# Attention in front of two expert layers: last rows, last key chunk and softmax factors as 128x128 tiles, and a scheduler that counts changes of TensorE's tiling

## The chip, the cores and the metric

One Trainium2 chip, one core, one launch. The metric is the device time in microseconds of one execution of the whole program. Four engines compute: TensorE (PE), VectorE (DVE), ScalarE (ACT) and GpSimd (POOL); SyncE (SP) issues most of the transfers. Each engine takes its own instructions in program order and waits on semaphores for the others.

## The reference

Three layers in a row, all float32. The attention is local softmax attention mixed with a memory read; its output is the input of a mixture of experts, whose output goes through a gated layer.

```python
B, H, S, D = 4, 8, 576, 64
scores = where(causal, -1e9, q @ k.T / sqrt(D));  scores -= scores.max(-1)
a = exp(scores);  a /= a.sum(-1) + 1e-9
local = a @ v
q_p = phi(q)                                  # phi(x) = where(x > 0, x, exp(x) - 1) + 1
mem = (q_p @ M_prev) / (q_p . z_prev + 1e-6)
out = g * mem + (1 - g) * local               # g = sigmoid(beta), one per head
x = moe(out as 2304 rows of 512)              # 8 experts, one per row, width 1024
y = (sigmoid(x @ w_gate) * (x @ w_val)) @ w_out   # width 1536
```

## The kernel before, in words

**Attention** works on 16 pairs of heads (`pi` 0 to 15; two pairs make a load group `gi`). A head has 576 rows: four chunks of 128 and a last one of 64. The last 64 rows of two heads are laid on the two halves of the partitions of one 128x128 tile; the two pairs of a load group stand side by side in an array of 18 blocks of 64 columns, whose last 128 columns (`1024:1152`) hold the last rows of pair `l` in the partitions `64*l` to `64*l+63`. Per pair, the steps are:

- `turn` (L309 to L322): q, k and phi(q) are transposed on TensorE, chunks 0 to 2 as group 0, chunks 3 and 4 as group 1. Chunks of 128 rows are 128x128 transposes (L316), the last one uses 64 partitions only (L320), the half that belongs to the pair. `q_part`, `z_part`, `k_part`, `p_part` take the result out of PSUM, q and k as a high part (ACT) and a low part (DVE).
- `scores` (L368): for chunks 0 to 3 of the rows, two heads side by side, each with 64 contraction rows (L378, six matmuls); for the last rows both heads at once with 128 contraction rows (L385).
- `masked` and `exp`: DVE masks and takes the maximum out of PSUM (L407), ACT exponentiates and sums (L415).
- `turn_probs`, `keep_probs`: 128x128 transposes of the probabilities (L460), copied out of PSUM by ACT or DVE (L304, L306). The last key chunk gives 64 rows.
- `recip`, `rc_turn`, `rc_copy`, `fan`: 1/sum of each row (18 columns: nine high, nine low) is transposed (L432) into `rT` of 18 partitions and spread over the partitions by matmuls with a selecting matrix `pick` of 18 contraction rows (L444, L446).
- `out_part` (L494): probabilities times v, the two heads writing the two halves of the output partitions, 64 weight columns each; the last key chunk has 64 contraction rows. `mem_part` (L480) reads the memory. `out_scale`, `out_add` (DVE) combine.

So TensorE is used in several **tilings**: whole (128x128), two row halves (64 contraction rows: L378, L320), two column halves (64 output partitions: L494), column halves on 64 rows (L494's last chunk), 18 rows (L444, L446), and 32 columns (L833, the router's logits).

**Order.** The order of all steps, on all engines, is made by a list scheduler (`Plan`, L55). A step has a rank, a cost for each engine that may run it, needs, and buffers that it takes and uses. `order` picks again and again the ready step with the smallest key: first the earliest start in steps of 0.02 us by the planner's own clock, then the rank. Instructions are then issued in the order of those starts. Buffers set waits: two PSUM tiles for scores (`Sp`), four for all else (`T`).

**After attention** come the routing (ranks of the rows by expert, lists of row numbers), a gather of the first rows from memory, the experts' loop and the gated layer; these have orders of their own that no edit here touches. While attention runs, the first experts' weights are already loaded and split.

Of the kernel before, what the change touches and what calls it, by code (L numbers as in the profile page):

```python
# [20 lines left out]
HG = 4  # L21
# [31 lines left out]
def chunk_rows(c):  # L53
    return 128 if c < 4 else 64


class Plan:
# [8 lines left out]
    SAME = {"PE": 0.0, "DV": 0.13, "PL": 0.1, "AC": 0.06, "SP": 0.0, "Q": 0.0}  # L66

    def __init__(self, bufs, later, step):


        self.bufs, self.later, self.step, self.steps, self.users = bufs, later, step, {}, {}

    def add(self, name, rank, cost, fn, needs=(), takes=(), uses=()):

        assert name not in self.steps, name
        self.steps[name] = (rank, cost, fn, tuple(needs), tuple(takes))
        for t in (*takes, *uses):
            self.users.setdefault(t, []).append(name)

    def order(self):  # L80
# [6 lines left out]
        ready, out = [n for n, w in waits.items() if not w], []  # L87
# [10 lines left out]
        while ready:  # L98
            best = None
            for n in ready:  # L100
# [4 lines left out]
                for e, c in cost.items():  # L105
                    t = max([free.get(e, 0.0), *t0, *(end[m][0] + (self.SAME if end[m][1] == e and (e != "SP" or n[0] == "ld") else self.LAG)[end[m][1]] for m in needs)])
                    b_ = self.later.get(e, 0.0) if len(cost) > 1 else 0.0
                    key = (n != "cp", round((t + b_) / self.step), rank, t + c + b_)
# [4 lines left out]
            end[n], free[e] = (t + c, e), t + c  # L113
            for tag, key in self.steps[n][4]:
# [12 lines left out]
class Attention:  # L127
# [14 lines left out]
    def constants(self, beta):  # L142
# [4 lines left out]
        self.rb = cp.tile([P, S], F32, name="rb")  # L147
        self.qT = [cp.tile([P, 2, 512], F32R, name=f"qT{i}") for i in range(2)]
# [48 lines left out]
        self.pt = [cp.tile([P, 2, NK, S], F32, name=f"pt{i}") for i in range(2)]  # L197

    def choices(self):

        nc, cp, n = self.nc, self.cp, 2 * NQ
        f = self.pt[1].rearrange("p h k q -> p (h k q)")[0:n, 0 : 6 * P].rearrange("p (c m) -> p c m", m=P)
        nc.gpsimd.memset(f, 0.0)
# [8 lines left out]
        self.pick = cp.tile([n, 6, P], F32R, name="pick")  # L212
        nc.gpsimd.tensor_copy(self.pick, f)
# [42 lines left out]
    def load_v(self, gi):  # L256
        b, h0 = gi // 2, (gi % 2) * HG
        self.G[gi, "v"] = vn = self.ld.tile([P, NK, HG, D], F32, name="vn", tag="vn")
        for hh in range(HG):
# [4 lines left out]
            out=vn[:64, 4, :, :], in_=self.v[b, h0 : h0 + HG, 512:576, :].rearrange("h p d -> p h d")  # L264
# [43 lines left out]
    def turn(self, nm, pi, g):  # L308
# [4 lines left out]
        for c in self.GROUPS[g]:  # L313
# [4 lines left out]
            else:  # L318
                r = slice(l * 64, (l + 1) * 64)
                nc.tensor.transpose(T[:, n : n + 64], src[r, 1024:1152], self.ident[r, r])  # L320
                n += 64
        self.T[nm, pi, g] = T, self.GROUPS[g][0] * 128, n  # L322

# [10 lines left out]
    def z_part(self, pi, lo):  # L334

        z, T = self.z8[pi % 2], self.T["q", pi, 1][0]
        for j in range(2):
            r = slice(j * 64, j * 64 + 64)
            v = T[r, 128:192]
# [5 lines left out]
    def k_part(self, pi, g, lo):  # L345
# [3 lines left out]
        T, c0, n = self.T["k", pi, g]  # L349
        if lo:  # L350
            self.nc.vector.tensor_tensor(  # L351
                kz[:, 1, c0 : c0 + n], T[:, :n], kz.bitcast(F32)[:, 0, c0 : c0 + n], ALU.subtract
            )
        else:
# [1394 lines left out]
```

## Time and profile before

| what | us |
|---|---|
| three runs, median (lowest to highest) | 1106.94 (1103.66 to 1111.6) |
| the profiled execution, device time | 1110.49 |
| its span, first to last instruction | 1108.6 |
| TensorE busy in the span | 1028.2 (93%) |
| VectorE / ScalarE / GpSimd busy | 525.0 / 456.2 / 289.1 |

The rows of the profile below come from that one execution; 1.9 us of its time lie outside the span. TensorE's matmuls are pipelined, so the time of one row reaches into the next: what a group of matmuls costs is read from the start of its row to the start of the next row. An fp32 matmul can stand as two instructions, so counts in the trace can be twice those in the order.

### The profile page before, as it was taken

The page shows a single profiled execution, that of the slowest core. Times are in us where ns is not written, and L with a number is a line of the kernel's source. Part 1 is how long each engine was busy: PE and PEld are TensorE (multiplying, and loading weights), DVE is VectorE, ACT ScalarE, POOL GpSimd, SP SyncE. Part 2 cuts the span into 40 slices and gives each one's busy share as a digit, 9 for nine tenths or more (in the row PEclk, how much of TensorE's full clock was granted, in tenths as well). Part 3 has the DMA queues.
Part 4 walks back from the last instruction along what each step waited for, and adds up shares of the span by engine and source line. Part 5 has one row for each costly group of instructions (what it writes and reads, how often), then busy time and mean ns, then how long its engine had stood idle before and what let it go on. Part 6 is the DMA issues. An engine that isn't in the chain of part 4 may idle for free. (4 is left out here: it accounts for less than half of the span.)

```text
span 1108.6 us, 17069 instructions
## 1 busy us (share of the span) xinstructions
PE 1028.2 (93%) x6181; PEld 878.6 (79%) x6181; DVE 525.0 (47%) x1263; ACT 456.2 (41%) x1049; POOL 289.1 (26%) x396
## 2 busy tenths in 40 slices
PE   6899899999869699989979789999999999999997
PEld 4567566666559589968968689999899999999996
DVE  5877677676564163246216799931212122121111
ACT  5687686876444253236224455521212221221211
POOL 8677446231374152035115200000100100100101
PEclk9899999999879899999999889999999999999999
DMA  6637445321277164138225455500110100100000
GB/s 123 130 99 172 104 85 131 73 66 36 75 261 257 44 236 136 39 91 295 73 66 149 162 175 196 159 1 1 38 48 1 58 1 1 57 1 1 30 1 28
DMA packets 111899, 102.49 MB, mean 92 GB/s; under 512 B 69520, under 2 KB 86928, under 8 KB 111760
## 3 DMA queue, kind: packets, MB, share of 16 engines
q1 hardware_dynamic: 107888, 88.18, 27.7%
q0 software_dynamic: 3872, 12.62, 3.6%
q8 instruction: 68, 1.11, 0.4%
q14 instruction: 71, 0.58, 0.2%
HBM read 84.49 MB, written 16.28 MB: 91 GB/s over the span
## 5 line engine op out<-in xcount | busy, mean ns | idle before, releaser
L1546 DVE TENSOR_TENSOR G<-G,pT 128x384 f32<-128x384 f32 (+1 forms) x74 | 40.1, 542 | 249.0 <-PE pT L1532 247.5
L1578 POOL DMA_INDIRECT out_dram<-o,rows x18 | 17.5, 971 | 461.7 <-ACT o L1574 212.5
L1553 ACT ACTIVATE Gh<-G 128x384 fp32r<-128x384 f32 (+1 forms) x74 | 38.2, 516 | 162.1 <-DVE G L1546 162.0
L1542 ACT ACTIVATE G<-pH 128x384 f32<-128x384 f32 x72 | 35.4, 491 | 132.4 <-PE pH L1532 132.3
L415 ACT ACTIVATE Sm<-Sm,mx 128x512 f32<-128x512 f32 (+3 forms) x144 | 83.2, 579 | 14.1 <-DVE mx L407 13.6
L407 DVE CUSTOM_DVE_ANT_0 Sm<-Sp,mask 128x512 f32<-128x512 f32 (+3 forms) x144 | 65.2, 481 | 19.6 <-PE T L460 8.1
L1166 POOL TENSOR_TENSOR W<-raw,W 128x1024 fp32r<-128x1024 f32 (+1 forms) x25 | 56.7, 2274 | 66.8 <-ACT W L1159 66.8
L460 PE MATMUL T<-ident,Sm 128*128 128x128 f32 (+1 forms) x400 | 61.2, 287 | 8.9 <-ACT xt L304 3.2
L1563 PE MATMUL pX<-W,Gh 128*128 128x512 f32 x220 | 68.9, 394 | 0.0
L1159 ACT ACTIVATE W<-raw 128x1024 fp32r<-128x1024 f32 x60 | 61.7, 1054 | 13.8 <-DMA y_dram<-y 6.5
L460 PEld LDWEIGHTS T<-ident,Sm 128*128 128x128 f32 (+1 forms) x400 | 44.3, 142 | 21.0 <-ACT xt L304 4.0
L1166 DVE TENSOR_TENSOR W<-raw,W 128x1024 fp32r<-128x1024 f32 x38 | 56.9, 1508 | 6.8 <-ACT W L1159 6.8
L494 PE MATMUL O<-pt,vn 128*64 128x192 f32 (+4 forms) x512 | 59.7, 353 | 0.0
L304 ACT ACTIVATE pt<-T 128x512 f32<-128x512 f32 (+4 forms) x128 | 49.3, 434 | 24.5 <-PE T L460 24.0
L1551 DVE TENSOR_TENSOR Gl<-G,Gh 128x384 fp32r<-128x384 f32 (+1 forms) x74 | 40.4, 546 | 33.9 <-ACT Gh L1553 33.9
L1532 PE MATMUL pT<-xh,W 128*128 128x384 f32 x264 | 52.8, 343 | 2.0 <-DVE G L1546 2.0
L1532 PE MATMUL pT<-yh,W 128*128 128x384 f32 x264 | 51.3, 336 | 0.0
L378 PE MATMUL Sp<-kz,qT 64*128 64x512 f32 (+3 forms) x384 | 49.0, 361 | 1.9 <-DVE kz L351 0.8
L1532 PEld LDWEIGHTS pT<-xh,W 128*128 128x128 f32 x264 | 47.4, 192 | 3.0 <-DVE G L1546 2.2
L1297 PE MATMUL pH<-W,xh 128*128 128x512 f32 x80 | 26.4, 472 | 24.8 <-issue 24.3
L1532 PE MATMUL pH<-yh,W 128*128 128x384 f32 x240 | 47.0, 337 | 1.4 <-DVE xl L1521 1.4
L494 PEld LDWEIGHTS O<-pt,vn 128*64 128x64 f32 (+1 forms) x512 | 30.6, 137 | 21.6 <-issue 13.7
(336 smaller groups left out, 2457.8 us busy)
## 6 DMA issues: line engine op xcount, KB each, us to landing
raw<-in_moe_w_dram SPq DMA_DIRECT2D x60, 512.0 KB, 5.1
raw<-in_moe_w_gate_dram SPq DMA_DIRECT2D x12, 512.0 KB, 5.9
raw<-in_moe_w_val_dram SPq DMA_DIRECT2D x12, 512.0 KB, 3.7
raw<-in_moe_w_out_dram SPq DMA_DIRECT2D x12, 512.0 KB, 4.6
y_dram<-y SPq DMA_DIRECT2D x9, 513.0 KB, 3.5
qn<-in_q_dram SPq DMA_DIRECT2D x32, 128.0 KB, 2.6
kn<-in_k_dram SPq DMA_DIRECT2D x32, 128.0 KB, 2.7
zf<-in_z_prev_dram SPq DMA_DIRECT2D x32, 128.0 KB, 5.3
```

Of the source, the lines that this page charges most:

```text
L304: self.nc.scalar.activation(out, in_, AF.Copy)
L378: nc.tensor.matmul(Sp[:, j, 0:n], lhsT=q[r, a, c * 128 : (c + 1) * 128], rhs=kz[r, k, 0:n], start=(p_ == 0), stop=(p_ == 2), skip_group_ch ...
L407: self.nc.vector.tensor_tensor_reduce(out=self.Sm[pi, n][:, k0:k1], in0=self.Sp[pi, c][:, j if n < 8 else si, 0 : k1 - k0], in1=mask, scal ...
L415: self.nc.scalar.activation(self.Sm[pi, n], self.Sm[pi, n], AF.Exp, scale=-1.0, bias=self.mx[pi, n][:, si : si + 1], accum_out=self.sums[p ...
L460: nc.tensor.transpose(T[:kr, o * 128 : (o + 1) * 128], self.Sm[pi, n][:, i * 128 : i * 128 + kr], self.ident)
L494: nc.tensor.matmul(O[j * 64 : (j + 1) * 64, q0 - q0b : q1 - q0b], lhsT=self.G[gi, "v"][:kr, i, 2 * l + j, :], rhs=PT[:kr, j, i, q0:q1], st ...
L1159: self.nc.scalar.activation(hi, t, AF.Copy)
L1166: eng.tensor_tensor(lo[:, o : o + w], t[:, o : o + w], hi.bitcast(F32)[:, o : o + w], ALU.subtract)
L1532: nc.tensor.matmul(t, lhsT=w[:, k * P : (k + 1) * P], rhs=x[:, k, :], start=(m == k == 0), stop=(m == 2 and k == 3),)
L1546: nc.vector.tensor_tensor(t, t, p, ALU.mult)
L1551: nc.vector.tensor_tensor(l, t, hi.bitcast(F32), ALU.subtract)
L1563: nc.tensor.matmul(po[g][jj], lhsT=a[:, ts], rhs=w, start=(f == 0 and m == 0), stop=(f == NF - 1 and m == 2), skip_group_check=True,)
```

## The change

Three things are done together.

1. **Whole square tiles.** The transposes of the last rows take all 128 partitions, both pairs of the load group at once, and the pair's 64 columns are picked when PSUM is read (`turned`). So group 1 of a turn needs both halves of the load, and a copy of k or phi(q) of group 1 becomes two (128 columns and 64). The last key chunk becomes keys 448 to 575: `vn`'s chunk 4 holds 128 rows of v, the transposed probabilities keep rows 64 to 127, and rows 0 to 63 of that chunk are zeros, set once. The softmax factors' tile `rc` is 128x128 with zeros, `rT` has 128 partitions, `pick` 128 rows.
2. **Scheduler.** A TensorE step has a `mode` (0 whole, 1 row halves, 2 column halves, 3 logits). A step of another mode than the last one costs 0.12 us more in the planner and stands two ranks later.
3. **Needs.** The products `("o", pi, bk, 0)` now need the fan `("b", pi, bk)` of the same block; `recip` needs `pick`; group 1 of a turn needs load half 1.

```diff
@@ class Plan
+    CHANGE = 0.12
+    WORTH = 2.0
...
-                    key = (n != "cp", round((t + b_) / self.step), rank, t + c + b_)
+                    new = e == "PE" and self.modes[n] != tiling
+                    c += self.CHANGE * new
+                    key = (n != "cp", round((t + b_) / self.step), rank + self.WORTH * new, t + c + b_)
...
+            if e == "PE":
+                tiling = self.modes[n]
@@ constants, choices
+        self.rcs = [cp.tile([P, P], F32, name=f"rc{i}") for i in range(2)]
+        self.rT = cp.tile([P, P], F32R, name="rT")
...
+        for t in self.pt:
+            nc.gpsimd.memset(t[0:64, :, 4, 512:576], 0.0)
...
-        self.pick = cp.tile([n, 6, P], F32R, name="pick")
+        self.pick = cp.tile([P, 6, P], F32R, name="pick")
...
@@ load_v
-            out=vn[:64, 4, :, :], in_=self.v[b, h0 : h0 + HG, 512:576, :].rearrange("h p d -> p h d")
+            out=vn[:, 4, :, :], in_=self.v[b, h0 : h0 + HG, 448:576, :].rearrange("h p d -> p h d")
@@ turn
-                r = slice(l * 64, (l + 1) * 64)
-                nc.tensor.transpose(T[:, n : n + 64], src[r, 1024:1152], self.ident[r, r])
+                nc.tensor.transpose(T[:, n : n + 128], src[:, 1024:1152], self.ident)
...
+    def turned(self, nm, pi, g):
+        T, c0, n = self.T[nm, pi, g]
+        if g == 0:
+            return [(c0, T[:, :n])]
+        o = 128 + pi % 2 * 64
+        return [(c0, T[:, :128]), (c0 + 128, T[:, o : o + 64])]
@@ k_part (p_part alike)
-            self.nc.scalar.activation(kz[:, 0, c0 : c0 + n], T[:, :n], AF.Copy)
+        for c0, v in self.turned("k", pi, g):
+            c = slice(c0, c0 + v.shape[1])
+            if lo:
+                self.nc.vector.tensor_tensor(kz[:, 1, c], v, kz.bitcast(F32)[:, 0, c], ALU.subtract)
+            else:
+                self.nc.scalar.activation(kz[:, 0, c], v, AF.Copy)
@@ rc_turn, rc_copy
-        self.nc.tensor.transpose(T[0 : 2 * NQ, 0:P], self.rc[pi], self.ident)
+        self.nc.tensor.transpose(T[:, 0:P], self.rcs[pi % 2], self.ident)
...
-        self.copy(eng, self.rT[pi], self.TR[pi][0 : 2 * NQ, 0:P])
+        self.copy(eng, self.rT, self.TR[pi][:, 0:P])
@@ turn_probs, out_part
-            nc.tensor.transpose(T[:kr, o * 128 : (o + 1) * 128], self.Sm[pi, n][:, i * 128 : i * 128 + kr], self.ident)
+            k0 = min(i * 128, S - 128)
+            nc.tensor.transpose(T[:, o * 128 : (o + 1) * 128], self.Sm[pi, n][:, k0 : k0 + 128], self.ident)
...
-                O[j * 64 : (j + 1) * 64, q0 - q0b : q1 - q0b], lhsT=self.G[gi, "v"][:kr, i, 2 * l + j, :],
-                rhs=PT[:kr, j, i, q0:q1], start=(i == 0), stop=(i == last), skip_group_check=True,
+                O[j * 64 : (j + 1) * 64, q0 - q0b : q1 - q0b], lhsT=self.G[gi, "v"][:, i, 2 * l + j, :],
+                rhs=PT[:, j, i, q0:q1], start=(i == 0), stop=(i == last), skip_group_check=True,
@@ run
-                        needs=[("L", nm, gi, pi % 2)] + (before if nm == "q" else [("X", "k", pi, 0)] if g else []),
+                        needs=[("L", nm, gi, 1 if g else pi % 2)] + (before if nm == "q" else [("X", "k", pi, 0)] if g else []),
...
-                    needs = [("o", pi, bk, i - 1)] if i else [("L", "v", gi)]
+                    needs = [("o", pi, bk, i - 1)] if i else [("L", "v", gi), ("b", pi, bk)]
```

The costs that the planner gives to the split copies stay as they were.

The order of TensorE at the start of the program, before. `qn`, `kn` are loaded q and k, `Sp` scores, `Sm` probabilities, `T` a PSUM tile.

```order
L316 MATMUL T<-ident,qn 128x128 x4
L320 MATMUL T<-ident,qn 128x64
L316 MATMUL T<-ident,kn 128x128 x4
L320 MATMUL T<-ident,kn 128x64
L378 MATMUL Sp<-kz,qT_104 128x512 x6
L378 MATMUL Sp<-kz,qT_104 128x128 x6
L316 MATMUL T<-ident,qn 128x128 x4
L320 MATMUL T<-ident,qn 128x64
L460 MATMUL T<-ident,Sm 128x128 x4
```

The same place now:

```order
L330 MATMUL T<-ident,qn 128x128 x3
L330 MATMUL T<-ident,kn 128x128 x3
L330 MATMUL T<-ident,qn 128x128
L334 MATMUL T<-ident,qn 128x128
L330 MATMUL T<-ident,qn 128x128 x4
L334 MATMUL T<-ident,qn 128x128
L330 MATMUL T<-ident,kn 128x128
L334 MATMUL T<-ident,kn 128x128
L330 MATMUL T<-ident,kn 128x128 x4
L334 MATMUL T<-ident,kn 128x128
L399 MATMUL Sp<-kz,qT_107 128x512 x6
L399 MATMUL Sp<-kz,qT_107 128x128 x6
```

The first scores of the first pair stood behind that pair's transposes alone; now they stand behind the transposes of two pairs, the last of which read the second half of the load of k.

TensorE around the products of the second pair, before. `rT`, `pick` are the fan's tiles, `vn` is v, `pt` the transposed probabilities, `phT` and `MB` the memory read.

```order
L444 MATMUL T<-rT,pick 128x128 x4
L446 MATMUL T<-rT,pick 128x64 x2
L378 MATMUL Sp<-kz,qT_105 128x256 x6
L494 MATMUL O<-pt_147,vn 64x384 x2
L494 MATMUL O<-pt_147,vn 64x256 x2
L494 MATMUL O<-pt_147,vn 64x128 x2
L480 MATMUL O<-phT,MB 128x384
L494 MATMUL O<-pt_147,vn 64x192 x8
L494 MATMUL O<-pt_147,vn 64x64 x2
L460 MATMUL T<-ident,Sm 128x128 x10
```

And now:

```order
L464 MATMUL T<-rT,pick 128x128 x4
L466 MATMUL T<-rT,pick 128x64 x2
L330 MATMUL T<-ident,kn 128x128 x3
L330 MATMUL T<-ident,qn 128x128 x4
L334 MATMUL T<-ident,qn 128x128
L399 MATMUL Sp<-kz,qT_107 128x512 x6
L514 MATMUL O<-pt_150,vn 64x384 x2
L514 MATMUL O<-pt_150,vn 64x256 x2
L514 MATMUL O<-pt_150,vn 64x128 x2
L514 MATMUL O<-pt_150,vn 64x192 x8
L514 MATMUL O<-pt_150,vn 64x64 x2
L480 MATMUL T<-ident,Sm 128x128 x9
```

The products L494 of a pair, split by the memory read and with a last part on 64 rows, are now one run (L514) behind the pair's fan, and the fan stands among whole-tile steps.

## Rows read from the trace of the kernel before

**Rows 1.** The page's busy time, share of the span and instructions by engine.

```profile
PE 1028.2 (93%) x6181; PEld 878.6 (79%) x6181; DVE 525.0 (47%) x1263; ACT 456.2 (41%) x1049; POOL 289.1 (26%) x396
```

**Rows 2.** Busy time by stretch: PE, PEld, DVE, ACT, POOL, granted clock, DMA.

```profile
24.00:40.00 16.00, 13.14 (x97) 9.13 (x94) 15.29 (x53) 14.48 (x46) 7.44 (x11) 1.00 0.70 120
160.00:180.00 20.00, 19.91 (x164) 14.20 (x163) 15.98 (x59) 15.32 (x48) 8.02 (x11) 1.00 0.55 119
24.00:295.00 271.00, 255.14 (x1945) 177.25 (x1942) 196.55 (x673) 188.72 (x578) 128.07 (x173) 0.98 0.42 96
```

**Rows 3.** TensorE's timeline in mid-attention: start, us, line, output and inputs, weights, shape.

```profile
101.56 1.31 PE L460 MATMUL T<-ident,Sm 128*128 128x128 f32 x10
102.80 0.55 PE L378 MATMUL Sp<-kz,qT 64*128 64x128 f32 x6
...
103.71 0.27 PE L316 MATMUL T<-ident,qn 128*128 128x128 f32 x1
103.92 0.27 PE L320 MATMUL T<-ident,qn 64*128 64x64 f32 x1
104.12 0.33 PE L316 MATMUL T<-ident,kn 128*128 128x128 f32 x1
104.38 0.27 PE L320 MATMUL T<-ident,kn 64*128 64x64 f32 x1
104.58 0.55 PE L316 MATMUL T<-ident,ph 128*128 128x128 f32 x3
```

**Rows 4.** TensorE's timeline, three runs of scores and the rows behind them.

```profile
28.00 1.15 PE L378 MATMUL Sp<-kz,qT 64*128 64x384 f32 x12
29.08 0.55 PE L316 MATMUL T<-ident,kn 128*128 128x128 f32 x3
...
105.52 0.79 PE L378 MATMUL Sp<-kz,qT 64*128 64x384 f32 x6
106.25 0.33 PE L316 MATMUL T<-ident,ph 128*128 128x128 f32 x1
...
110.65 0.62 PE L378 MATMUL Sp<-kz,qT 64*128 64x256 f32 x6
111.20 0.55 PE L460 MATMUL T<-ident,Sm 128*128 128x128 f32 x3
```

**Rows 5.** TensorE's timeline where lines alternate and the tiling stays whole.

```profile
108.81 0.49 PE L460 MATMUL T<-ident,Sm 128*128 128x128 f32 x3
109.13 0.60 PE L930 MATMUL T<-ident,xT 128*128 128x128 f32 x4
109.57 0.49 PE L460 MATMUL T<-ident,Sm 128*128 128x128 f32 x3
```

**Rows 6.** Timeline at the start of the program, TensorE and SP's transfers.

```profile
8.22 0.79 PE L378 MATMUL Sp<-kz,qT 64*128 64x512 f32 x2 [0.42 <-ACT kz L355]
9.80 1.76 PE L378 MATMUL Sp<-kz,qT 64*128 64x512 f32 x10 [0.78 <-DVE kz L351]
...
16.08 0.61 SPq L227 DMA_DIRECT2D kn<-in_k_dram  x1
...
18.08 1.97 PE L378 MATMUL Sp<-kz,qT 64*128 64x384 f32 x12
19.98 1.12 PE L316 MATMUL T<-ident,kn 128*128 128x128 f32 x4
```

**Rows 7.** ScalarE's groups by shape, 24 to 295 us: busy, mean ns of one.

```profile
L304 ACT ACTIVATE pt<-T 128x128 f32<-128x128 f32 x24 | 5.5, 280 | 0.3 <-PE T L460 0.2
L343 ACT ACTIVATE z<-T 64x64 fp32r<-64x64 f32 x28 | 6.0, 213 | 0.2
L355 ACT ACTIVATE kz<-T 128x192 fp32r<-128x192 f32 x14 | 4.6, 328 | 0.4 <-PE T L320 0.4
```

**Rows 8.** Timeline, TensorE: the fan that waited longest.

```profile
118.72 0.52 PE L444 MATMUL T<-rT,pick 18*128 18x128 f32 x3 [1.24 <-DVE xt L306]
```

**Rows 9.** Timeline, TensorE: the first rows of the first expert.

```profile
308.76 1.09 PE L1270 MATMUL pX<-ident,xn 128*128 128x128 f32 x4 [3.25 <-DMA xn<-x_dram,kept]
```

## The prediction before the run

> **What bounds the kernel now.** I read the page first: TensorE is busy 93% of the span, no other engine half of it [rows 1]. Then the stretches. In attention, from 24 to 295 us, TensorE is busy 255.1 of 271 us, at a granted clock of 0.98, VectorE 196.6 and ScalarE 188.7, GpSimd 128.1; in a full stretch such as 160 to 180 TensorE stands at 19.91 of 20 [rows 2]. So attention is TensorE's, with one exception: from 24 to 40 us VectorE is busy 15.29 of 16 and TensorE only 13.14 [rows 2]. Behind attention comes a chain that waits for the last row of x: the first expert's transposes wait 3.25 us for the gathered rows [rows 9]. Nothing in the change touches that chain or what follows, so a microsecond won before 295 us should arrive at the end, and one lost too. The work is therefore to price attention on TensorE, then ask what the other engines give back.
>
> **What a change of tiling costs.** A group's cost is read from its start to the next row's start. Where lines alternate but the tiling stays whole, three transposes take 109.13 − 108.81 = 0.32 us and four 0.44, that is 0.107 to 0.11 each, so a new line or tile costs nothing [rows 5]. Ten transposes between two groups of scores take 102.80 − 101.56 = 1.24 us against 10 x 0.107 = 1.07: 0.17 for going in and out [rows 3]. The scores' side pays as well: widths 384 and 256 in one run take 29.08 − 28.00 = 1.08 us, apart 0.73 + 0.55 = 1.28, so 0.20 for the second out and in [rows 4]. A run of scores merged with another and the transposes between merged too saves both, 0.37 for two changes. The worst place is group 1 of the turns: whole, half, whole, half, each one transpose, from 103.71 to 104.58, 0.87 us [rows 3]. Two whole ones are 0.21; for a half one no row shows its time without the changes. It lies between 0 and 0.107, the time of a whole one; I take half, 0.053. That leaves 0.87 − 0.32 = 0.55 for four changes, 0.14 each. So the price lies between 0.085 (only the 0.17, for two) and 0.185 (0.37 for two); I take 0.14, which is also the place that the edit removes most often.
>
> **What the change removes.** Counted along TensorE's order from the first instruction to the first expert, changes between whole, row halves, column halves, 18 rows and 32 columns fall from 328 to 146. In the order of before alone, whole squares would take away 92 (the transposes of last rows 71, the fans 7, the last key chunk 14); the rest, 90, is the scheduler's: products in one run, scores behind scores. 182 x 0.14 = 25.5 us (15.5 to 33.7). The transposes of last rows get wider, 48 x 0.053 = 2.6 us back (0 to 5.1 by the bound above). Transposing `rc` whole and giving the fan and the last keys 128 contraction rows leaves the count of moving columns as it was: 0 for these, as far as the changes they caused are counted above. TensorE: −22.9 us.
>
> **What it adds.** First, the start. Scores of the first pair now need k of group 1, which needs the second half of the load. SP issues the last piece of that load at 16.08 us and the transposes that read it start at 19.98 [rows 6], against scores at 8.22 now. What TensorE did of scores before that moment, 0.79 + 1.76 + 1.97 = 4.5 us [rows 6], comes later. It costs no less than the same runs at mid-attention's speed (about half: four transposes take 1.12 us in rows 6, 0.60 in rows 5), 2.3 us, and no more than the whole shift, 19.98 − 8.22 = 11.8. VectorE, the engine that is full from 24 to 40 us, starts its masks late as well, so nothing catches up soon, but the present start also loses time waiting for the same load. I take 4.5.
>
> Second, the split copies: k high on ScalarE, k low on VectorE, phi(q) on either, one more for each of 16 pairs, 48 in all. On ScalarE 192 columns take 328 ns; 128 columns take 280 and a 64x64 piece 213 [rows 7]: 165 ns more, 48 x 0.165 = 7.9 us over two engines. They have room on average (196.6 and 188.7 of 271), but k's copies stand between its transposes and the scores. Between 0 and 7.9; half, 3.9.
>
> Third, a wait. The first product of a block now stands behind its fan, and the fan behind all nine exponentials, the reciprocal, a transpose and a copy. Queued behind it are the transposes of the next probabilities, and the copies that they feed. The longest such wait shown is 1.24 us [rows 8]. If all 16 pairs had it, 19.8 us; if the scheduler finds other whole-tile work each time, 0. I take two of that length, 2.4.
>
> More zeros to set on GpSimd and 64 more rows of v in a load of 128 KB are hidden: GpSimd is busy 128.1 of 271 us [rows 2] and v is loaded ahead of its use.
>
> **Sum.** −22.9 + 4.5 + 3.9 + 2.4 = −12.1 us. Against the profiled execution, 1110.49 (span 1108.6 and 1.9 outside), that is 1098.4. That execution lies 3.55 us above the median of 1106.94, so against the median I say **1094.8 us**, 1.1% faster.
>
> **Rivals.** *The copies become the bound.* VectorE and ScalarE together do 196.6 + 188.7 + 7.9 = 393.2 us in attention, 1.42 us per us now. Their fullest stretch under a saturated TensorE reaches 15.98 + 15.32 of 20, 1.565 [rows 2]. If no more than 1.5 can be held, attention takes 262 us instead of 271: 9 saved, less 4.5 at the start, so 4.4 and 1102.5 us. For it: from 24 to 40 us TensorE already waits for a full VectorE. Against it: on average each has over a quarter of its time free. The Trainium skill has this as a rule (TensorEngine Tiling (Array Packing), Performance Considerations, PSUM Bottleneck): what speeds TensorE up doesn't speed up emptying PSUM, which may become the bottleneck. Rows 2 bear it out for 24 to 40 us and not for 160 to 180.
>
> *The full price.* If a change costs 0.185 as two merged runs suggest, TensorE saves 31.1, and with the same 10.8 given back the gain is 20.3: 1086.6 us. For it: the second instruction behind a change is late too, which the single transposes can't show.
>
> *Slower: products wait for the fan.* Place: the first product of each pair. Price: 1.24 us in each of 16 pairs, 19.8, with the 8.4 of start and copies 28.2 against 22.9: 5.3 slower, 1112.2 us. It decides from (22.9 − 8.4) / 16 = 0.9 us per pair on. For it: the chain from the last exponential to the fan crosses three engines. Against it: one wait of 1.24 is the longest shown, and the new order puts the transposes of k, q or further scores between fan and products.
>
> *The edit doesn't do what it says*, if the time belonged to something else than the tiling, such as weights of a new tile: then fewer changes buy nothing, and only the 10.8 remain. Rows 5 speak against it, where the tile and line change four times without a price; I leave it inside the slower case.
>
> **How the numbers follow.** Forecast 0.50 (by itself 1088 to 1101), copies 0.20, full price 0.22, slower 0.08. The time is the forecast's. The range takes in the full price and the copies: **1084 to 1107**. About 1% is what a measurement of this kernel can tell from no change: below 1095.9 is faster, above 1118.0 slower. Faster is the full price and a little over half of the forecast, 0.22 + 0.28 = 0.50; slower by over 1% needs the fan's wait and the dearest start together, some part of the 0.08 and of the unknown, 0.07; the rest, 0.43, is no change that can be told.
>
> **What would show it.** Right: single transposes of last rows 0.107 us apart with no jump; products in runs; attention's last transposes some 12 us earlier; the first scores at 20 to 21 us. Wrong: a TensorE row of waits for VectorE or ScalarE well above the present 16 us idle between 24 and 295 (the copies or the fan), waits in front of the first product of a pair, or a jump at line changes in whole tiling. If the stretch behind attention changed by itself, the step that carries the gain to the end would be wrong.

## The result and the profile after

The changed kernel takes **1090.11 us**, median of 6 runs (1087.83 to 1094.44), beside 1107.15 (1103.66 to 1111.6) for the kernel before: ratio 0.9863 [0.9833, 0.9892], 17.0 us less by the medians. The forecast was 1094.8, 12.1 less. All ratios here leave out one slower run, 1113.38 us, of the kernel `order_k_first` below. The profiled execution of the new kernel took 1087.83 us, its span is 1085.8.

The page of the changed kernel, busy time by engine, against [rows 1]:

```profile
PE 1000.4 (92%) x6181; PEld 874.5 (81%) x6181; DVE 518.0 (48%) x1275; ACT 458.4 (42%) x1079; POOL 296.9 (27%) x410
```

TensorE has as many instructions as before and 27.8 us less of busy time. Where that lies is read from one landmark: the router's `T<-O,tri`, the first step that needs all of attention. It starts at 294.29 us before:

```profile
294.29 0.45 PE L951 MATMUL T<-O,tri 128*128 128x144 f32 x2
```

TensorE's timeline of the changed kernel, the places that answer to [rows 3], [rows 6], [rows 8] and [rows 9]:

```profile
15.39 0.45 PE L334 MATMUL T<-ident,qn 128*128 128x128 f32 x1 [8.15 <-DMA qn<-in_q_dram]
...
18.50 0.47 PE L334 MATMUL T<-ident,kn 128*128 128x128 f32 x1 [1.39 <-DMA kn<-in_k_dram]
...
19.98 2.18 PE L399 MATMUL Sp<-kz,qT 64*128 64x512 f32 x12
...
24.41 2.39 PE L480 MATMUL T<-ident,Sm 128*128 128x128 f32 x10
26.73 0.62 PE L399 MATMUL Sp<-kz,qT 64*128 64x256 f32 x6
...
28.18 0.49 PE L330 MATMUL T<-ident,qn 128*128 128x128 f32 x3
28.50 0.49 PE L330 MATMUL T<-ident,kn 128*128 128x128 f32 x3
...
41.42 0.27 PE L334 MATMUL T<-ident,qn 128*128 128x128 f32 x1
41.53 0.27 PE L330 MATMUL T<-ident,kn 128*128 128x128 f32 x1
41.64 0.27 PE L334 MATMUL T<-ident,kn 128*128 128x128 f32 x1
41.84 1.13 PE L399 MATMUL Sp<-kz,qT 64*128 64x128 f32 x12
...
251.79 0.66 PE L464 MATMUL T<-rT,pick 128*128 128x128 f32 x4
252.29 0.36 PE L466 MATMUL T<-rT,pick 128*128 128x64 f32 x2
252.58 2.93 PE L514 MATMUL O<-pt,vn 128*64 128x384 f32 x32
255.44 1.20 PE L480 MATMUL T<-ident,Sm 128*128 128x128 f32 x9
...
277.42 0.45 PE L971 MATMUL T<-O,tri 128*128 128x144 f32 x2
...
291.73 1.09 PE L1290 MATMUL pX<-ident,xn 128*128 128x128 f32 x4 [3.09 <-DMA xn<-x_dram,kept]
```

The transposes of last rows (L334) start 0.11 us apart, where the half ones stood 0.2 to 0.26 apart in [rows 3]. The products are one run behind the fan, and the fan waits for nothing there. The first scores come at 19.98 us; the long wait in front of them, 8.15 us, is for the second half of q, the one for k is 1.39. Attention ends at 277.42, 16.87 us earlier, and the first expert follows 17.03 earlier than in [rows 9], with nearly the same wait for its rows (3.09 us, 3.25 before).

Windows of the kernel before, up to its end of attention, and two stretches in which its granted clock fell (columns as in [rows 2]):

```profile
0.00:24.00 24.00, 13.59 (x62) 10.31 (x63) 12.25 (x54) 10.77 (x30) 20.06 (x64) 1.00 0.66 125
24.00:294.30 270.30, 254.71 (x1944) 176.96 (x1941) 196.00 (x672) 188.12 (x576) 127.45 (x172) 0.98 0.42 96
...
36.00:50.00 14.00, 12.09 (x68) 8.60 (x67) 10.58 (x39) 10.86 (x34) 11.67 (x15) 0.76 0.74 118
248.00:260.00 12.00, 9.50 (x66) 6.41 (x63) 7.95 (x33) 6.06 (x19) 5.22 (x10) 0.86 0.39 94
```

The changed kernel, its own end of attention and the stretches of [rows 2], and two that an experiment below is set against:

```profile
24.00:40.00 16.00, 14.21 (x104) 11.07 (x102) 13.58 (x54) 14.43 (x48) 8.97 (x14) 1.00 0.80 129
160.00:180.00 20.00, 19.04 (x158) 14.61 (x157) 14.31 (x55) 16.23 (x50) 9.74 (x16) 1.00 0.65 163
0.00:24.00 24.00, 8.19 (x38) 6.23 (x38) 10.66 (x45) 7.91 (x22) 21.23 (x69) 1.00 0.68 129
24.00:277.40 253.40, 236.42 (x1968) 180.66 (x1964) 191.66 (x692) 193.02 (x614) 129.67 (x182) 1.00 0.44 104
60.00:100.00 40.00, 37.20 (x312) 28.63 (x312) 33.09 (x113) 31.21 (x104) 29.21 (x39) 1.00 0.65 155
...
24.00:60.00 36.00, 31.43 (x242) 23.47 (x238) 29.43 (x109) 30.90 (x100) 26.72 (x36) 1.00 0.71 131
```

From these rows attention's end can be split into three: idle time of TensorE (length less busy), what the lower clock costs, and the rest, the work. Before, TensorE is busy 13.59 + 254.71 = 268.3 us to the end and idle 10.4 before 24 us and 15.6 after. A granted clock of 0.76 is a mean of the two levels, 2.4 and 1.2 GHz, so twice the missing share stands at 1.2: 14 x 0.24 x 2 + 12 x 0.14 x 2 = 10.1 us of attention. Half of that, 5.1, is charged to the clock, so the work is 263.2. Now TensorE is busy 244.6 us, idle 15.8 before and 17.0 after, and by the clock's column never at the low level. In [rows 2]'s stretches VectorE is no longer full from 24 to 40 us (13.58 of 16, TensorE 14.21), and from 160 to 180 TensorE has lost some of its cover (19.04 for 19.91).

So −16.9 is made of **work −18.6, start +5.4, later idle +1.4, clock −5.1**.

The column misses the start. It says 1.00 there, but in the changed kernel ten transposes from 24.41 us on take 0.23 us each and those from 28.18 on 0.107; before, four take 1.12 us in [rows 6] and 0.60 in [rows 5]. TensorE's first stretch runs at half pace in all kernels here, before up to about 23 us, now up to about 27. TensorE is busy some 13 and 11 us of it. If that pace is the low level's, about 1 us of the gain belongs to the clock and not to the work: −17.4 and −6.2. In the table below the same reading moves work by −0.4 to +1.4 us, and by 3 to 4 for half_first, k_first_warm and order_k_first.

TensorE's waits in attention, after: what it waited for, total us, times, longest. Others are left out, among them those at the start and smaller ones.

```profile
PE T L334 <- DMA qn<-in_q_dram: 8.1, 1, 8.1
...
PE T L480 <- DVE xT L524: 3.2, 4, 1.6
PE T L330 <- DVE xT L530: 2.7, 2, 2.2
PE Sp L406 <- DVE mx L428: 2.6, 3, 1.0
...
PE T L480 <- DVE kz L374: 0.9, 2, 0.6
```

No wait stands in front of a pair's first product (L514), and those for the copies of k (`kz`) are below 1 us each. ScalarE's groups by shape, 24 to 277.4 us, against [rows 7]:

```profile
L376 ACT ACTIVATE kz<-T 128x128 fp32r<-128x128 f32 x14 | 3.9, 277 | 3.0 <-PE T L334 2.9
...
L376 ACT ACTIVATE kz<-T 128x64 fp32r<-128x64 f32 x14 | 3.2, 228 | 0.0
```

A split copy of k takes 277 + 228 − 328 = 177 ns more than the whole one. Whether TensorE pays for it, even_copies below asks.

### The profile page after: what moved, and what is told of

Same layout as the page of the kernel before. It is cut to its first block, busy times and chain, and to the rows that moved or that the text cites. A ratio compares the mean times of both kernels' runs of the same rounds, so it can differ in the third digit from the quotient of the medians.

```text
span 1085.8 us, 17186 instructions
## 1 busy us (share of the span) xinstructions
PE 1000.4 (92%) x6181; PEld 874.5 (81%) x6181; DVE 518.0 (48%) x1275; ACT 458.4 (42%) x1079; POOL 296.9 (27%) x410
## 5 line engine op out<-in xcount | busy, mean ns | idle before, releaser
L1186 POOL TENSOR_TENSOR W<-raw,W 128x1024 fp32r<-128x1024 f32 (+1 forms) x25 | 59.9, 2400 | 58.5 <-ACT W L1179 58.4
L428 DVE CUSTOM_DVE_ANT_0 Sm<-Sp,mask 128x512 f32<-128x512 f32 (+3 forms) x144 | 64.5, 482 | 15.6 <-PE T L480 6.8
L480 PE MATMUL T<-ident,Sm 128*128 128x128 f32 x400 | 62.7, 285 | 7.8 <-DVE xT L524 3.2
L318 ACT ACTIVATE pt<-T 128x512 f32<-128x512 f32 (+4 forms) x138 | 55.9, 447 | 32.0 <-PE T L480 30.8
L1179 ACT ACTIVATE W<-raw 128x1024 fp32r<-128x1024 f32 x60 | 61.5, 1054 | 12.1 <-DMA y_dram<-y 4.6
L480 PEld LDWEIGHTS T<-ident,Sm 128*128 128x128 f32 x400 | 44.7, 143 | 21.2 <-DVE xT L524 4.9
L1317 PE MATMUL pH<-W,xh 128*128 128x512 f32 x80 | 26.5, 473 | 23.4 <-issue 22.7
L399 PE MATMUL Sp<-kz,qT 64*128 64x512 f32 (+3 forms) x384 | 46.2, 354 | 1.7 <-DVE mx L428 1.6
L514 PE MATMUL O<-pt,vn 128*64 128x192 f32 (+4 forms) x512 | 47.1, 336 | 0.0
L1552 PEld LDWEIGHTS pT<-yh,W 128*128 128x128 f32 x264 | 46.4, 188 | 0.8
```

The source lines that it names most:

```text
L318: self.nc.scalar.activation(out, in_, AF.Copy)
L399: nc.tensor.matmul(Sp[:, j, 0:n], lhsT=q[r, a, c * 128 : (c + 1) * 128], rhs=kz[r, k, 0:n], start=(p_ == 0), stop=(p_ == 2), skip_group_ch ...
L428: self.nc.vector.tensor_tensor_reduce(out=self.Sm[pi, n][:, k0:k1], in0=self.Sp[pi, c][:, j if n < 8 else si, 0 : k1 - k0], in1=mask, scal ...
L480: nc.tensor.transpose(T[:, o * 128 : (o + 1) * 128], self.Sm[pi, n][:, k0 : k0 + 128], self.ident)
L514: nc.tensor.matmul(O[j * 64 : (j + 1) * 64, q0 - q0b : q1 - q0b], lhsT=self.G[gi, "v"][:, i, 2 * l + j, :], rhs=PT[:, j, i, q0:q1], start= ...
L1179: self.nc.scalar.activation(hi, t, AF.Copy)
```

## Experiments

Twelve kernels ran. Each has its edit against the changed kernel, if no other is named. The table gives all: changes of tiling on TensorE from the first instruction to the first expert, median and ratio to the kernel before on the same chip, and for the profiled execution the end of attention less that of before, split as above (work + idle + clock). The clock is charged half of all time at 1.2 GHz, which is too much where TensorE also waits, so work reads some us low where the clock term is large. One profile stands behind each split, six to twelve runs (after_again: five) behind each median.

| kernel | changes | median us | ratio [95%] | end − 294.3 = work + idle + clock |
|---|---|---|---|---|
| before | 328 | | 1 | 0 |
| after | 146 | 1090.11 | 0.9863 [0.9833, 0.9892] | −16.9 = −18.6 + 6.8 − 5.1 |
| after_again | 146 | 1089.32 | 0.9855 [0.983, 0.988] | −15.4 = −18.5 + 4.8 − 1.7 |
| squares_alone | 226 | 1106.32 | 0.9988 [0.9962, 1.0013] | −4.5 = −8.6 + 7.5 − 3.4 |
| squares_need | 177 | 1106.2 | 0.9984 [0.9958, 1.001] | +0.2 = −15.1 + 10.1 + 5.2 |
| order_alone | 242 | 1088.55 | 0.9827 [0.9798, 0.9855] | −18.5 = −12.5 − 2.6 − 3.4 |
| price_only | 187 | 1099.24 | 0.9929 [0.9901, 0.9957] | −5.1 = −15.0 + 8.1 + 1.8 |
| half_turns | 212 | 1095.36 | 0.9881 [0.9853, 0.9909] | −14.5 = −13.6 + 2.5 − 3.4 |
| all_small | 248 | 1096.73 | 0.9921 [0.9898, 0.9944] | −10.4 = −8.4 + 1.4 − 3.4 |
| even_copies | 146 | 1092.59 | 0.9885 [0.9859, 0.9911] | −16.7 = −17.8 + 6.2 − 5.1 |
| k_first | 141 | 1094.03 | 0.9893 [0.9869, 0.9918] | −12.8 = −21.1 + 1.4 + 6.9 |
| half_first | 143 | 1096.89 | 0.991 [0.9878, 0.9942] | −14.1 = −21.5 + 3.9 + 3.5 |
| k_first_warm | 141 | 1107.23 | 1.0005 [0.9984, 1.0027] | −9.0 = −17.2 + 3.1 + 5.2 |
| order_k_first | 237 | 1105.31 | 0.9974 [0.9947, 1.0001] | −5.3 = −16.4 − 0.8 + 12.0 |

### The tiles without the scheduler's terms, and the order without the tiles

squares_alone: whole squares, the scheduler blind to tilings, and the products free of the fan.

```diff
-    CHANGE = 0.12
-    WORTH = 2.0
+    CHANGE = 0.0
+    WORTH = 0.0
...
-                    needs = [("o", pi, bk, i - 1)] if i else [("L", "v", gi), ("b", pi, bk)]
+                    needs = [("o", pi, bk, i - 1)] if i else [("L", "v", gi)]
```

> The changed kernel with the scheduler's price and rank penalty set to 0 and without the products' need of the fan: whole squares alone. Changes of tiling in the order: 226 (before 328, changed 146). Theory (each change costs TensorE 0.14 to 0.165 us; wider transposes 2.6, late start 4.5, copies 3.9 come back): 102 changes fewer, -14.3 to -16.8 + 11.0 = 3 to 6 us faster than before, 1101 to 1104. Rival 'the gain is the scheduler's': squares alone lose their 11 us less a little, 1110 or more. Rival 'fewer stalls, not fewer changes': no relation to the count; no change, 1107.

squares_need: the same with the need for the fan kept.

```diff
-    CHANGE = 0.12
-    WORTH = 2.0
+    CHANGE = 0.0
+    WORTH = 0.0
```

> As the changed kernel, but price and rank penalty 0: whole squares and the need of the fan. 177 changes. Theory: 151 fewer, -21.1 to -24.9, + 2.6 + 4.5 + 3.9 + 2.4 = 8 to 11.5 us faster than before, 1095.5 to 1099. Rival 'the gain is the scheduler's': 1107 or more. Rival 'the need of the fan costs a wait per pair': slower than the squares alone.

order_alone: the tiles of the kernel before (their lines put back in `turn`, `k_part`, `p_part`, `rc_turn`, `rc_copy`, `fan`, `turn_probs`, `out_part`, the loads and the needs of group 1); modes, terms and the fan's need stay. The larger terms find no order with these tiles.

```diff
-    CHANGE = 0.12
-    WORTH = 2.0
+    CHANGE = 0.06
+    WORTH = 1.5
...
-                nc.tensor.transpose(T[:, n : n + 128], src[:, 1024:1152], self.ident)
+                r = slice(l * 64, (l + 1) * 64)
+                nc.tensor.transpose(T[:, n : n + 64], src[r, 1024:1152], self.ident[r, r])
```

> The kernel of before with its own tiles, plus the scheduler's modes, price 0.06 and rank penalty 1.5 (0.12 and 2.0 find no order here) and the need of the fan. 242 changes, no late start, no split copies, no wider transposes. Theory: 86 fewer, -12 to -14.2 + 2.4 for the fan = 9.6 to 11.8 us faster than before, 1095.5 to 1097.5. Rival 'squares are what counts': within 3 us of before, 1104 to 1107.

Measured: the squares alone 0.9988, with the need 0.9984, neither told from the kernel before; the order alone 0.9827, whose interval overlaps that of the whole change. So an order alone can bring the whole gain, and across orders the count of changes doesn't decide: 151 fewer bring nothing, where 8 to 11.5 us were expected, and 86 fewer bring 19.2 us (1107.77 − 1088.55), where 9.6 to 11.8 were. The need of the fan stands in squares_need and order_alone alike, so it isn't what differs. The windows say where it goes. order_alone to its end of attention:

```profile
0.00:24.00 24.00, 13.65 (x69) 9.86 (x69) 12.62 (x57) 10.82 (x31) 20.09 (x64) 1.00 0.73 127
24.00:275.80 251.80, 238.73 (x1937) 176.38 (x1933) 183.92 (x655) 187.95 (x583) 129.51 (x182) 0.99 0.47 103
```

And squares_need, with the stretch 60 to 100 us:

```profile
0.00:24.00 24.00, 8.68 (x39) 6.33 (x40) 10.96 (x45) 8.40 (x24) 20.96 (x68) 1.00 0.69 130
24.00:294.50 270.50, 249.66 (x1964) 188.81 (x1964) 197.96 (x712) 190.01 (x589) 130.36 (x184) 0.96 0.44 97
60.00:100.00 40.00, 33.02 (x237) 25.64 (x237) 30.48 (x92) 25.69 (x84) 30.96 (x41) 0.87 0.65 154
```

Two of its waits, total us, times, longest:

```profile
PE T L480 <- DVE xT L530: 3.2, 1, 3.2
...
PE T L330 <- DVE qT L352: 2.5, 1, 2.5
```

squares_need saves 15.1 us of TensorE's work and hands all of it back: 36.2 us idle where before had 26.0, and a clock of 0.96. From 60 to 100 us TensorE does 237 instructions at 0.87, the changed kernel 312 at 1.00; both waits above, for VectorE's step on `xT` and for its copy of q, lie in that stretch, and the clock falls within 1 us behind the end of either. order_alone saves less work, 12.5, and idles less than before, with its start as early as before. Against it the changed kernel saves 6.1 us more of work (250.7 − 244.6), and its start loses 5.5 (13.65 − 8.19 of busy time before 24 us): in this pair the whole squares pay for their late start and no more. The pair isn't the change with one part left out, as the terms are 0.06 and 1.5 here; all_small below divides the change itself.

price_only: the planner still counts 0.12 us for a change, but the rank no longer moves.

```diff
-    WORTH = 2.0
+    WORTH = 0.0
```

> The changed kernel with the planner's price of 0.12 kept and the rank penalty 0: 187 changes, ten more than the squares with the fan's need (177, 1106 us, which counted no price). Theory 'the number of changes decides': 1107, 1 slower than with 177. Theory 'a planner that knows the price places the steps so that TensorE waits less and keeps its clock': 1090 to 1098, with idle time after 24 us near 15 and fewer half-clock stretches than the 20.5 us there. In between, 1099 to 1104, neither alone.

Measured 0.9929, between: its interval touches neither that of the changed kernel (0.9833 to 0.9892) nor that of squares_need (0.9958 to 1.001). Knowing the price and preferring the same tiling each seem to give a part. Its work is −15.0, the same as squares_need; what differs is idle time and clock.

### The price of a change, at one order

half_turns: the order of the changed kernel step for step, with the transposes of last rows on 64 partitions again.

```diff
-                nc.tensor.transpose(T[:, n : n + 128], src[:, 1024:1152], self.ident)
+                r = slice(l * 64, (l + 1) * 64)
+                nc.tensor.transpose(T[:, n + l * 64 : n + (l + 1) * 64], src[r, 1024:1152], self.ident[r, r])
```

> The changed kernel, the same order on every engine, but the transposes of the last rows use 64 partitions again (same needs, same split copies, same start): 212 changes instead of 146, the transposes half as wide. This is the price of a change by itself. Theory: 66 x 0.14 to 0.165 = 9.2 to 10.9, less 48 x 0.053 = 2.6: 6.7 to 8.3 us slower than the changed kernel, 1097 to 1098.5. Rival 'fewer stalls, not fewer changes': the same as the changed kernel within 2 us, 1088 to 1092.

all_small: besides, the fan on 18 contraction rows and the last key chunk on 64.

```diff
-            nc.tensor.matmul(T[:, o : o + P], lhsT=self.pick[:, n], rhs=r, start=True, stop=True, skip_group_check=True)
+            nc.tensor.matmul(T[:, o : o + P], lhsT=self.pick[0 : 2 * NQ, n], rhs=r[0 : 2 * NQ], start=True, stop=True, skip_group_check=True)
...
+        r = slice(128 - chunk_rows(i), 128)
...
-                rhs=PT[:, j, i, q0:q1], start=(i == 0), stop=(i == last), skip_group_check=True,
+                rhs=PT[r, j, i, q0:q1], start=(i == 0), stop=(i == last), skip_group_check=True,
```

> The changed kernel's order, needs, start and copies, but every tile small again: transposes of last rows and products of the last keys on 64 partitions, the fan on 18. 248 changes of tiling instead of 146, the transposes half as wide. Theory (0.116 us of TensorE per change, as the busy times of the five kernels run so far give): 102 x 0.116 - 2.6 = 9.2 us more TensorE time, 1099 us. Rival 'the price hides behind other waits': under 3 us slower, 1090 to 1093. If the price were 0.165: 14 us slower, 1104.

after_again: the changed kernel, no edit, on the same chip as all_small.

> The changed kernel unchanged, as the reference of this group: 1090 us, faster than before by 1.4 to 1.7%.

all_small against after_again on one chip, 0.9921 against 0.9855 with intervals that don't meet: 1096.73 − 1089.32 = 7.4 us for 102 more changes, 0.073 each in time. So of the 15.7 us that the change brings on this chip (before 1105.04, less 1089.32), 7.4 need the whole tiles and 8.3 stay with small ones in the same order. In TensorE's work, all_small and then after_again:

```profile
0.00:24.00 24.00, 9.01 (x39) 6.34 (x40) 10.79 (x45) 8.38 (x24) 20.66 (x68) 1.00 0.68 130
24.00:283.90 259.90, 247.53 (x1964) 182.50 (x1964) 191.94 (x692) 193.42 (x611) 129.49 (x182) 0.99 0.42 101
```

```profile
0.00:24.00 24.00, 8.41 (x38) 6.23 (x38) 10.82 (x45) 8.12 (x22) 21.07 (x68) 1.00 0.60 130
24.00:278.90 254.90, 239.66 (x1966) 184.32 (x1964) 191.75 (x692) 193.46 (x613) 129.16 (x182) 0.99 0.44 103
```

254.8 − 244.7 = 10.1 us of work, plus the 2.6 that narrower transposes are estimated to spare, over 102: **0.125 us** a change. half_turns gives 249.6 − 244.6 = 5.0, plus 2.6, over 66: **0.115**; its medians differ by 5.3 us, but its ratio's interval overlaps that of the changed kernel. The 2.6 is the prediction's estimate, with bounds of 0 and 5.1 us, which no run measured; with these the prices are 0.10 to 0.15 and 0.08 to 0.15. The Trainium skill (TensorEngine Tiling (Array Packing), Key Properties) says that a change of tiling mode drains TensorE; it gives no price. These runs agree that a change costs TensorE time, about 0.12 us each; that the time is a drain, no run shows by itself. Time shows less than the work because TensorE's waits shrink: after 24 us it idles 259.90 − 247.53 = 12.4 us in all_small, 15.2 in after_again.

### The copies and the start

even_copies: for even pairs the 192 columns lie together, and one copy takes them: 24 copies fewer, the order as it is.

```diff
+        if pi % 2 == 0:
+            return [(c0, T[:, :n])]
```

> The changed kernel with one copy instead of two for group 1 of k and phi(q) in even pairs (there the columns are contiguous): 24 copies fewer of 48, the planner's order unchanged. If the split copies cost 3.9 us together, as the prediction took: 2 us faster, 1088. If they lie beside other work: 1090.

Measured 0.9885 beside 0.9855 for after_again, intervals overlapping: no gain shown. That the split copies cost anything on the path is not shown.

k_first: the loads of z, M and v of the first group wait until k's second half is issued.

```diff
...
-            add(("L", "v", gi), r + 3, {"SP": 3.3}, lambda e, g=gi: self.load_v(g), takes=[("vn", gi)])
+            add(("L", "v", gi), r + 3, {"SP": 3.3}, lambda e, g=gi: self.load_v(g), needs=[("L", "k", 0, 1)] * (gi == 0), takes=[("vn", gi)])
```

> The changed kernel with the loads of z, M and v of the first group needing the second half of the first k load, so that SP issues the halves of q and k first; 141 changes. Theory 'late start': first scores near 12 us instead of 20, about 5 us of TensorE's idle time before 24 us gone, 1085 us. Rival 'VectorE sets the first 40 us anyway, or z and v come late': 1089 to 1092.

half_first: q and k of the first pair alone use half transposes and need their own half of the load.

```diff
-                nc.tensor.transpose(T[:, n : n + 128], src[:, 1024:1152], self.ident)
+                if pi or nm == "ph":
+                    nc.tensor.transpose(T[:, n : n + 128], src[:, 1024:1152], self.ident)
+                else:
+                    nc.tensor.transpose(T[:, n : n + 64], src[0:64, 1024:1152], self.ident[0:64, 0:64])
...
-                        needs=[("L", nm, gi, 1 if g else pi % 2)] + (before if nm == "q" else [("X", "k", pi, 0)] if g else []),
+                        needs=[("L", nm, gi, 1 if g and pi else pi % 2)] + (before if nm == "q" else [("X", "k", pi, 0)] if g else []),
```

> The changed kernel, but q and k of the first pair alone use the old half transposes and need their own half of the load only; the start of TensorE's order is that of before again, 143 changes. Theory 'late start': first scores near 8 us, about 5 us less idle time before 24 us, 1084 to 1085 us. Rival (as the loads put first have shown) 'what is won at the start is given back by idle spells behind it and a lower clock': 1088 to 1094.

The first scores come at 13.44 and at 7.81 us, and still both kernels are slower than the changed one by the medians: 1094.03 and 1096.89 (the interval of k_first overlaps that of after_again, that of half_first touches it). half_first:

```profile
0.00:24.00 24.00, 13.27 (x71) 10.01 (x72) 14.41 (x60) 11.52 (x35) 20.42 (x68) 1.00 0.73 126
24.00:280.20 256.20, 237.03 (x1933) 181.64 (x1932) 189.33 (x675) 190.47 (x600) 131.09 (x187) 0.97 0.46 103
24.00:60.00 36.00, 30.24 (x224) 23.31 (x222) 31.12 (x105) 29.08 (x92) 26.71 (x35) 0.91 0.68 129
```

It wins 5.1 us of busy time before 24 us, most of it at the half pace of the start. From 24 to 60 its VectorE is busy 31.12 of 36, its clock is 0.91, and it does 224 instructions of TensorE where the changed kernel does 242 at 1.00. In the end it idles less (29.9 us beside 32.8), and has 17.1 us of attention behind the start at the low clock, where the changed kernel has none. So the late start is a price that can be removed at its place and comes back elsewhere.

k_first_warm: k_first (against which the edit is shown) with spare work for TensorE, two more transposes of the identity before each group of `turn_probs` of the first three pairs. Nothing reads them.

```diff
+        for _ in range(2 if pi < 3 else 0):
+            nc.tensor.transpose(T[:, 0:128], self.ident, self.ident)
```

> The kernel with q's and k's loads first (1094 us), plus two spare 128x128 transposes of the identity in front of each group of probability transposes of the first three pairs, overwritten by what follows; 30 groups or so, 6.4 us of TensorE work at the upper level. Theory 'idle spells take the clock down': the half-clock stretches between 31 and 86 us (20.5 us in its profile) mostly go, 1087 to 1092, faster than without the spare work. Rival 'the clock is not what counts': 4 to 6 us slower than 1094.

order_k_first: order_alone with k_first's loads of z, M and v; one of the three lines is shown.

```diff
-            add(("L", "z", gi), r + 2, {"SP": 2.7}, lambda e, g=gi: self.load_z(g), takes=[("zf", gi)])
+            add(("L", "z", gi), r + 2, {"SP": 2.7}, lambda e, g=gi: self.load_z(g), needs=[("L", "k", 0, 1)] * (gi == 0), takes=[("zf", gi)])
...
```

> The scheduler's part on small tiles (1088.5 us) with q's and k's loads first; 237 changes. Theory: the wait of 4.2 us for q's second half before 16 us goes, 1084 to 1087. Rival 'given back by idle spells and the clock': 1088 to 1093.

Both lose the gain or nearly all of it: 1.0005 and 0.9974. k_first_warm is some 12 us slower than k_first by the ratios, more than either theory allowed. Its spare work didn't hold the clock: 20.5 us of attention are at the low level, 23.9 in k_first. But it doesn't test the theory either, as the first fall comes in a wait that the spare work can't fill, for a later load of k, at 28 to 33 us:

```profile
PE T L334 <- DMA kn<-in_k_dram: 5.4, 2, 5.1
```

The wait at that place is 1.9 us in k_first and 4.0 in order_k_first, and is none in the changed kernel: what the first loads gain, a later load seems to lose. In k_first_warm's profiled execution attention still ends 9.0 us earlier than before, but what follows takes 1103.8 − 285.3 = 818.5 us, where before has 814.3 and k_first 810.8; 5.6 us of it are one wait of an expert's matmuls for the split of a weight, which ScalarE does. order_k_first is the clearest case of the clock, 24 to 60 us, with its wait for k:

```profile
24.00:60.00 36.00, 30.08 (x172) 21.37 (x172) 19.97 (x67) 22.30 (x68) 19.76 (x31) 0.72 0.76 134
```

```profile
PE T L323 <- DMA kn<-in_k_dram: 4.0, 1, 4.0
```

At 0.72, TensorE gets through 172 instructions; the clock falls inside that wait for k. Its total of 34.1 us at the low level is the largest of all kernels, and of 19 us that the order alone won, some 3 are left by the ratio. No kernel here is shown to be faster than both the changed one and order_alone.

## Why the prediction was right, and where not

**Right: the direction and the place.** Attention is TensorE's, at one order fewer changes make it shorter, and what is won there arrives at the end: 16.9 us by the landmark, 17.0 by the medians. The profiled pair differs by 22.7, as the part behind attention came out 808.4 us long (1085.8 − 277.4) beside 814.3 (1108.6 − 294.3). Nothing there was edited. In the other profiles of after's order it is 810.5 (after_again, 1089.4 − 278.9) to 812.4, so some 4 us differ between executions of one order. Whether all of the 5.9 is such scatter, one profile of before can't tell; it has a wait there that after hasn't, an expert's matmuls for the split of a weight on VectorE:

```profile
PE pH L1357 <- DVE W L1166: 2.3, 1, 2.3
```

**Mis-sized: the price of a change, 0.14.** The step "I take 0.14", from one place with four changes, was somewhat high: 0.115 and 0.125 at equal order, and (18.6 + 2.6) / 182 = 0.116 over the whole change, all with the prediction's own 0.053 for a half transpose. 182 of them are 21 to 23 us, not 25.5. The lower end, 0.085, and the upper, 0.185, held it; the rival "full price", 0.185, is out, as 0.15 is the most that the bounds allow.

**Mis-sized: what is given back, 10.8.** Start, copies and fan cost 6.8 us of idle time. The start's 4.5 was near the 5.4 that the rows show, and nearer to 4.3, with the 1 us that doing less at half pace gives back; the first scores at 20 us came out too, though the long wait was for q and not for k. The copies' 3.9 and the fan's 2.4 were to be 6.3; idle after 24 us grew by 17.0 − 15.6 = 1.4, no wait for the fan's products shows, and even_copies won nothing. The prediction's own condition for no wait, other whole-tile work between fan and products, fits the order at the second pair; at 251.79 us the products follow the fan at once and don't wait either. The rival "copies become the bound" took 1.5 us per us as the limit for VectorE and ScalarE together; they now run at (191.66 + 193.02) / 253.4 = 1.52 and TensorE is still busy 93% of that stretch. "Products wait for the fan" is out for this order.

**Missing: the clock and the rest of the order.** The sum held TensorE's clock at [rows 2]'s 0.98 and had no term for it; in the profiled pair it gave 5.1 us, for after_again against the same execution of before 1.7, so it is a term that moves from execution to execution. More important, the sum priced the order by its count of changes, "the rest, 90, is the scheduler's", and would have given squares_need, with 151 fewer, most of the gain. Its work did fall by 15.1 us, and none of it reached the end. What the sum left out is that an order also sets where TensorE waits: idle time differs by 13 us between orders (36.2 to 23.4, 5 of it before 24 us) that all do the same computation.

The terms of the forecast thus summed to −12.1 with errors of both signs: work 4.3 too large (−22.9 for −18.6), give-backs 4.0 too large (10.8 for 6.8), clock 5.1 missing; −12.1 + 4.3 − 4.0 − 5.1 = −16.9. That the total came as near as 5 us is in part luck: the first two errors cancel, and the same way of summing was 6 to 10 us off for squares_need and 7 to 10 for order_alone.

**Partly open: the clock.** Over the 14 profiles the clock falls 28 times in attention behind the start. In 23 of them it falls during a single wait of TensorE of 1.3 to 5.1 us or at most 2.4 us behind its end; in the other five several shorter waits stand there. In the kernel before, the stretch from 36 to 50 us has this one:

```profile
38.71 1.06 PE L460 MATMUL T<-ident,Sm 128*128 128x128 f32 x5 [1.57 <-DVE kz L351]
```

So the waits come first, for VectorE, ScalarE or a transfer, and the low clock makes what follows slower. The six kernels whose TensorE idles over 18 us after 24 us (squares_need, price_only, k_first, half_first, k_first_warm, order_k_first) have 13.7 to 34.1 us at the low level in attention, the others 0 to 10.2. Not every wait is followed by a fall: the changed kernel has one of 2.15 us at 187.7 us and stays at the upper level. What tells the two apart is open, and no run took away one such wait alone.

**Open: how far an order scatters.** Each setting of the scheduler gave one order. Making three first loads wait, and nothing else, gave the small tiles an order that is some 16 us slower, so a part of what the terms seem to win may be the luck of that one order; no run compares several orders with equally many changes.

## What to carry to other kernels

Price a change of tiling from the starts of neighbouring rows, and confirm it with a kernel that has the same order and other tiles: here about 0.12 us of TensorE, of which some 60% reached the end in the pair that tells them apart. When a scheduler is changed together with the tiles, run each alone before crediting either; the count of what was removed says what TensorE saves, and only idle time and granted clock say what arrives. Mending a late start is worth trying, and worth measuring to the end: here 5 us won before 24 us were lost again later in attention, in part to a wait for a later load.

## What was not expected of the hardware

The granted clock falls to 1.2 GHz inside stretches where TensorE is busy most of the time, behind waits of a few us, at places that differ from order to order: [rows 2]'s mean of 0.98 hid 0.76 from 36 to 50 us, and the rows above show 0.72 over 36 us in order_k_first with TensorE busy 30.08 of them. Over whole runs the mean of the granted clock goes from 0.974 in the changed kernel to 0.959 in order_k_first; as (1 − clock) x 2 x span, that is 57 and 90 us at the low level, without the start, which the record of the clock leaves out. Over four sets of 11 to 23 runs of the kernel before, the time rises by 0.26 to 0.46 us for each such us (correlation 0.55 to 0.82): a part of the spread between executions goes with it, and why it differs between runs of one kernel is open.
